# Constants moved to GpSimd, xn and y written in place, and the two result stores exchanged, in a one-token attention and MLP kernel

## The chip, the cores and the metric

One core of a Trainium2 chip. The metric is the device time of one execution in microseconds (us). Runs are compared with runs of the kernel before made in the same rounds on the same chip. The four jobs below ran on three chips (8, 3, 0 and 0), so runs of different jobs are compared through their ratios to the kernel before. Verdicts call a difference under 2% "same"; the differences here are about 1% at most, so what matters is the 95% interval of the ratio.

## The reference

One token `x` of 1024 values goes through a layernorm and then, side by side, through attention over the last 4096 positions of a cache (32 query heads, 4 key/value heads of 128) and through an MLP that normalises again.

```python
x = A_x
xn = _layernorm(x, axis=-1)
return x + _A_ref(xn, A_k_cache, A_v_cache, A_wq, A_wo) + _B_ref(xn, B_w1, B_b1, B_w2, B_b2)
```

Everything is bf16. With one token there is little arithmetic; the weights and the cache, 39.85 MB, have to be read.

## The kernel before

Each engine has its own list, and semaphores join them. SyncE issues all large loads in one queue: wq, K0, K1, w1, K2, K3, V, then w2 and wo into buffers that become free. GpSimd makes constants, VectorE does the layernorms, TensorE multiplies. The buffers are placed in SBUF, the memory that holds them, in the order in which they are asked for: some 40 small ones, then three large ones that nearly all loads write. A load counts as landed when the last increment of its semaphore is recorded, at 95.72 us for the last load here. PSUM is the memory in which TensorE leaves its sums (`PS` in the traces).

```python
    XNT = sb("XNT", [128, 8], dt.float32)
    XNTb = sb("XNTb", [128, 8], dt.bfloat16)
    # ... (cut: small buffers)
    KV = sb("KV", [128, HKV * W + HKV * NBLK * DH], dt.bfloat16)
    # ... (cut: views of KV)
    W1 = sb("W1", [128, KC * F], dt.bfloat16)
    WA = sb("WA", [128, KC * NQ], dt.bfloat16)
```

The opening on VectorE, after the sums of x and x*x:

```python
    DVE.mark(dve.tensor_scalar(out=XNT[:, :], in0=XT16[:, 0:8],
                               scalar1=msx[:, 2:3], scalar2=msx[:, 7:8],
                               op0=ALU.subtract, op1=ALU.mult))
    dve_dep()
    d_xn = DVE.mark(dve.tensor_copy(XNTb[:, :], XNT[:, :]))
    dve_dep()
    dve.wait_ge(POOL.sem, c_z)
    d_xz = DVE.mark(dve.tensor_copy(XZ[:, 96:9 * 97 - 1:97], XNTb[:, :]))
```

And the end:

```python
    act.wait_ge(ACT.sem, a_out)
    act.dma_start(out_row[:, 0:512], OUT[0:1, :]).then_inc(s_out[0], 16)
    sp.wait_ge(DVE.sem, d_out)
    sp.dma_start(out_row[:, 512:1024], OUT[32:33, :]).then_inc(s_out[1], 16)
    act.wait_ge(s_out[0], 16)
    sp.wait_ge(s_out[1], 16)
```

Of the kernel before, what the change touches and what calls it, by code (L numbers as in the profile page):

```python
# [4 lines left out]
dt = mybir.dt  # L5
ALU = mybir.AluOpType
ACTF = mybir.ActivationFunctionType
AX = mybir.AxisListType
# [37 lines left out]
def bass_parallel_sum__sliding_block_cached__mixer_channel_mlp__decode_kernel(  # L46
# [17 lines left out]
    INV_D = 1.0 / D  # L64
# [3 lines left out]
    pe, dve, act, pool, sp = nc.tensor, nc.vector, nc.scalar, nc.gpsimd, nc.sync  # L68
# [12 lines left out]
    s_out = [nc.alloc_semaphore(f"s_out{n}") for n in range(2)]  # L81

    PE = Track(nc, "S_PE")
    DVE = Track(nc, "S_DVE")
    ACT = Track(nc, "S_ACT")
    POOL = Track(nc, "S_POOL")

    def sb(name, shape, dtype):
        return nc.alloc_sbuf_tensor(name, shape, dtype)

    identb = sb("identb", [128, 128], dt.bfloat16)
    identf = sb("identf", [128, 128], dt.float32)
    onesf = sb("onesf", [128, 128], dt.float32)
    SELI = sb("SELI", [128, 32], dt.float32)
    REPL = sb("REPL", [128, 128], dt.bfloat16)
    SEL = sb("SEL", [32, 512], dt.bfloat16)
# [4 lines left out]
    SEL2 = sb("SEL2", [4, 2], dt.bfloat16)  # L101
    XTT = sb("XTT", [128, 256], dt.bfloat16)
    XT16 = sb("XT16", [128, 16], dt.float32)
    msx = sb("msx", [128, 8], dt.float32)
    XNT = sb("XNT", [128, 8], dt.float32)
    XNTb = sb("XNTb", [128, 8], dt.bfloat16)
    YT16 = sb("YT16", [128, 16], dt.float32)
    msy = sb("msy", [128, 8], dt.float32)
    EXPW = sb("EXPW", [128, 1], dt.float32)
    YTb = sb("YTb", [128, 8], dt.bfloat16)  # L110
    TT = sb("TT", [128, 1024], dt.float32)
    QMASK = sb("QMASK", [128, 4], dt.float32)
    QDB = sb("QDB", [128, 128], dt.bfloat16)
# [6 lines left out]
    MX4 = sb("MX4", [1, 128], dt.float32)  # L120
# [2 lines left out]
    PT = sb("PT", [128, 1024], dt.bfloat16)  # L123
    XZ = PT[:, 0:9 * 97 - 1]
    YZ = sb("YZ", [128, 9 * 97 - 1], dt.bfloat16)
    SELB = sb("SELB", [8, 2 * 97], dt.bfloat16)
    SUMP = sb("SUMP", [128, 1], dt.float32)
    REC = sb("REC", [32, 1], dt.float32)
# [8 lines left out]
    OUT = KV[0:33, 4 * D:4 * D + 512]  # L137
# [4 lines left out]
    PS = nc.alloc_psum_tensor("PS", [128, 8 * 512], dt.float32)  # L142
# [10 lines left out]
    out_row = out.rearrange("b s n -> (b s) n")  # L153
# [32 lines left out]
    def ahead_of_barrier(engine, n):  # L186
# [13 lines left out]
    act.dma_start(B1R[:, :], b1_rows).then_inc(s_b1, 16)  # L200
    act.dma_start(XB[0:2, :], A_x.rearrange("b s (o n) -> (b s o) n", o=2)).then_inc(s_b2, 16)
    act.dma_start(XB[2:4, :], b2_rows).then_inc(s_b2, 16)
    DVE.mark(dve.memset(PS[:, 0:4 * 512], 0.0))

    POOL.mark(pool.memset(identf[:, :], 0.0))
    pool.wait_ge(POOL.sem, POOL.cnt)
# [1 line left out]
        out=identf[:, :], in_=identf[:, :],  # L208
        pattern=[[-1, 128]], compare_op=ALU.not_equal, fill=1.0,
        base=0, channel_multiplier=1))  # L210
    c_onesf = POOL.mark(pool.memset(onesf[:, :], 1.0))
    POOL.mark(pool.memset(identb[:, :], 0.0))
    pool.wait_ge(POOL.sem, POOL.cnt)
    c_identb = POOL.mark(pool.affine_select(
        out=identb[:, :], in_=identb[:, :],
        pattern=[[-1, 128]], compare_op=ALU.not_equal, fill=1.0,
        base=0, channel_multiplier=1))
    POOL.mark(pool.memset(SEL[:, :], 0.0))
    pool.wait_ge(POOL.sem, POOL.cnt)
    c_sel = POOL.mark(pool.affine_select(  # L220
        out=SEL[:, :].rearrange("h (q p) -> h q p", q=4),
        in_=SEL[:, :].rearrange("h (q p) -> h q p", q=4),
        pattern=[[-1, 4], [1, 128]], compare_op=ALU.not_equal, fill=1.0,
        base=0, channel_multiplier=-4))
# [4 lines left out]
        out=MASK[:, :], in_=MASK[:, :], pattern=[[-REP, HKV]], compare_op=ALU.is_ge, fill=0.0,  # L229
        base=0, channel_multiplier=1))  # L230
    pool.wait_ge(POOL.sem, POOL.cnt)
    c_mask = POOL.mark(pool.affine_select(
        out=MASK[:, :], in_=MASK[:, :], pattern=[[REP, HKV]], compare_op=ALU.is_ge, fill=0.0,
        base=REP - 1, channel_multiplier=-1))
# [2 lines left out]
    c_selb = POOL.mark(pool.affine_select(  # L237
        out=SELB[:, :].rearrange("r (n m) -> r n m", n=2), in_=SELB[:, :].rearrange("r (n m) -> r n m", n=2),
        pattern=[[-16, 2], [-1, 97]], compare_op=ALU.not_equal, fill=1.0, base=0, channel_multiplier=16))
    POOL.mark(pool.memset(XZ[:, :], 0.0))  # L240
    c_z = POOL.mark(pool.memset(YZ[:, :], 0.0))
    c_lq = POOL.mark(pool.memset(LQ[:, :], 0.0))
# [7 lines left out]
    def dve_dep():  # L250
        dve.wait_ge(DVE.sem, DVE.cnt)

    def moments(ms, T16):

        n = DVE.mark(dve.tensor_reduce(
            out=ms[:, 0:2],
            in_=PS[:, 7 * 512: 7 * 512 + 16].rearrange("p (a k) -> p a k", a=2),
            axis=AX.X, op=ALU.add))
        dve_dep()
        DVE.mark(dve.tensor_scalar(out=ms[:, 2:4], in0=ms[:, 0:2],  # L260
                                   scalar1=INV_D, scalar2=None, op0=ALU.mult))
        dve_dep()
        DVE.mark(dve.tensor_tensor(out=ms[:, 4:5], in0=ms[:, 2:3], in1=ms[:, 2:3], op=ALU.mult))
        dve_dep()
        v = DVE.mark(dve.scalar_tensor_tensor(
            out=ms[:, 5:6], in0=ms[:, 3:4], scalar=EPS, in1=ms[:, 4:5],
            op0=ALU.add, op1=ALU.subtract))
        act.wait_ge(DVE.sem, v)
        a = ACT.mark(act.activation(out=ms[:, 6:7], in_=ms[:, 5:6], func=ACTF.Sqrt))
        dve.wait_ge(ACT.sem, a)  # L270
        DVE.mark(dve.reciprocal(out=ms[:, 7:8], in_=ms[:, 6:7]))
        dve_dep()
        return n
# [4 lines left out]
                           in_=XR[:, :].rearrange("p (r k) -> p k r", k=KC)))  # L278
# [3 lines left out]
    d_xsq = DVE.mark(dve.tensor_tensor(  # L282
        out=XT16[:, 8:16], in0=XT16[:, 0:8], in1=XT16[:, 0:8], op=ALU.mult))
    pe.wait_ge(DVE.sem, d_xsq)
    pe.wait_ge(POOL.sem, c_onesf)
    pe_sum1 = PE.mark(pe.matmul(PS[:, 7 * 512: 7 * 512 + 16], lhsT=onesf[:, :], rhs=XT16[:, 0:16]))  # L286
    dve.wait_ge(POOL.sem, c_identf)
    DVE.mark(dve.tensor_reduce(out=SELI[:, :], in_=identf[:, :].rearrange("p (i c) -> p c i", i=4),
                               axis=AX.X, op=ALU.add))
    dve_dep()  # L290
    DVE.mark(dve.tensor_reduce(out=QMASK[:, :], in_=identf[:, :].rearrange("p (t c) -> p t c", t=4),
                               axis=AX.X, op=ALU.add))
    DVE.mark(dve.tensor_copy(REPL[:, :].rearrange("p (i c) -> p i c", i=4),
                                      SELI[:, :].unsqueeze(1).to_broadcast([128, 4, 32])))
    dve.wait_ge(POOL.sem, c_identb)
    DVE.mark(dve.tensor_tensor(out=SEL2[:, :], in0=identb[0:4, 0:2], in1=identb[0:4, 2:4], op=ALU.add))
    dve.wait_ge(PE.sem, pe_sum1)
    moments(msx, XT16)
    DVE.mark(dve.tensor_scalar(out=XNT[:, :], in0=XT16[:, 0:8],
                               scalar1=msx[:, 2:3], scalar2=msx[:, 7:8],  # L300
                               op0=ALU.subtract, op1=ALU.mult))
    dve_dep()
    d_xn = DVE.mark(dve.tensor_copy(XNTb[:, :], XNT[:, :]))
    dve_dep()
    dve.wait_ge(POOL.sem, c_z)
    d_xz = DVE.mark(dve.tensor_copy(XZ[:, 96:9 * 97 - 1:97], XNTb[:, :]))
    DVE.mark(dve.tensor_copy(YT16[:, 0:8], XNTb[:, :]))
    dve_dep()
    d_ysq = DVE.mark(dve.tensor_tensor(  # L309
        out=YT16[:, 8:16], in0=YT16[:, 0:8], in1=YT16[:, 0:8], op=ALU.mult))  # L310
    pe.wait_ge(DVE.sem, d_ysq)
    pe_sum2 = PE.mark(pe.matmul(PS[:, 7 * 512: 7 * 512 + 16], lhsT=onesf[:, :], rhs=YT16[:, 0:16]))  # L312
    dve.wait_ge(PE.sem, pe_sum2)
    moments(msy, YT16)
    act.wait_ge(ACT.sem, ACT.cnt)
    ACT.mark(act.activation(out=EXPW[:, 0:1], in_=msy[:, 6:7], func=ACTF.Exp))
    d_y = DVE.mark(dve.tensor_scalar(
        out=YTb[:, :], in0=YT16[:, 0:8], scalar1=msy[:, 2:3], scalar2=msy[:, 7:8],
        op0=ALU.subtract, op1=ALU.mult))
    dve_dep()  # L320
    d_yz = DVE.mark(dve.tensor_copy(YZ[:, 96:9 * 97 - 1:97], YTb[:, :]))
    d_zs = DVE.mark(dve.memset(PS[:, 4 * 512:6 * 512], 0.0))



# [17 lines left out]
    def turn_k(g):  # L343
# [7 lines left out]
        out=QDB[:, :].rearrange("p (t c) -> p t c", t=4),  # L351
# [3 lines left out]
    last = pe.matmul(PS[:, 6 * 512: 6 * 512 + 128], lhsT=REPL[:, :], rhs=QDB[:, :], start=True, stop=True)  # L355
    pe_qx = PE.mark(last)
    dve.wait_ge(PE.sem, pe_qx)
    dve.wait_ge(POOL.sem, c_lq)
    act.wait_ge(PE.sem, pe_qx)
    act.wait_ge(POOL.sem, c_lq)  # L360
    d_lq = a_lq = None
# [34 lines left out]
    pe.wait_ge(DVE.sem, d_lq)  # L396
    pe.wait_ge(ACT.sem, a_lq)

    pe.wait_ge(DVE.sem, d_zs)
    k_blocks = KT.rearrange("p (g n b j a) -> p g n b j a", g=HKV, n=2, b=16, j=4, a=32)  # L400
    q_blocks = LQ[:, 0:2048].rearrange("p (g j m) -> p g j m", g=HKV, j=4)
    with nc.Fori(0, HKV, 1, engines=TENSOR) as g:
# [21 lines left out]
    for j, nj in enumerate(WO_CHUNKS):  # L424
# [19 lines left out]
        scalar1=-SCALE, scalar2=None, op0=ALU.mult))  # L444
    pe.wait_ge(DVE.sem, d_mx4)
    pe_nmb = PE.mark(pe.matmul(
        PS[:, 7 * 512 + 128: 7 * 512 + 129], lhsT=MX4[0:1, :], rhs=onesf[0:1, 0:1]))
    dve.wait_ge(PE.sem, pe_nmb)
    d_nmb = DVE.mark(dve.tensor_copy(NMB[:, :], PS[:, 7 * 512 + 128: 7 * 512 + 129]))  # L449
    act.wait_ge(DVE.sem, d_nmb)  # L450
# [30 lines left out]


    pe.wait_ge(s_b2, 32)
    pe.wait_ge(DVE.sem, d_nmb)
    for n in range(2):
        pe.matmul(ACC[n], lhsT=SEL2[:, n:n + 1], rhs=XB[:, :], start=True, stop=False)
# [4 lines left out]
    dve.wait_ge(PE.sem, pe_tot)  # L491
    DVE.mark(dve.reciprocal(out=REC[:, :], in_=PS[0:32, 512:513]))
    dve_dep()
    dve.wait_ge(POOL.sem, c_mask)
    DVE.mark(dve.tensor_scalar(out=RM[:, :], in0=MASK[:, :], scalar1=REC[:, 0:1], scalar2=None, op0=ALU.mult))
    dve_dep()

# [35 lines left out]
    c = 0  # L533
# [34 lines left out]
    d_out = DVE.mark(dve.tensor_copy(OUT[32:33, :], ACC[1]))  # L568
    act.wait_ge(s_fin, 1)
    a_out = ACT.mark(act.activation(out=OUT[0:1, :], in_=ACC[0], func=ACTF.Copy))  # L570
    act.wait_ge(ACT.sem, a_out)
    act.dma_start(out_row[:, 0:512], OUT[0:1, :]).then_inc(s_out[0], 16)
    sp.wait_ge(DVE.sem, d_out)
    sp.dma_start(out_row[:, 512:1024], OUT[32:33, :]).then_inc(s_out[1], 16)
    act.wait_ge(s_out[0], 16)
    sp.wait_ge(s_out[1], 16)

    return nc

# [27 lines left out]
```

## Time and profile before

| | before |
|---|---|
| time, median of the first 3 runs | 99.29 us |
| span of the profile | 98.1 us |
| last load landed | 95.72 us |
| first q matmul | 12.49 us |

The page of the kernel before: span, then busy time of each engine with its share and its number of instructions, then DMA queues (packets, MB, time of the packets as a share of 16 engines' span).

```profile
span 98.1 us, 1063 instructions
PE 68.3 (70%) x330; PEld 32.2 (33%) x330; DVE 37.1 (38%) x57; ACT 5.8 (6%) x11; POOL 6.7 (7%) x19
...
q8 instruction: 1, 0.02, 0.1%
...
q14 instruction: 1, 0.01, 0.0%
```

No engine is busy for more than 70% of the span; the queue of loads, shown in the prediction, is for 95.8%. Look at the last line too, which is easily passed over: one packet of a queue of kind "instruction". The trace's record of it has 8 KB at 77.9 us.

The timeline of the kernel before around the first use of x (start, length, engine and line, operation, in brackets the wait before it):

```profile
6.22 1.90 POOL L242 MEMSET LQ<- 128x2176 bf16 x1
...
7.65 0.63 DVE L277 STREAM_TRANSPOSE XTT<-XR 128x256 bf16<-128x256 bf16 x1 [4.40 <-DMA XR<-in_A_x_dram]
8.31 0.17 DVE L280 CAST XT<-XTT 128x8 f32<-128x8 bf16 x1
...
12.49 16.87 PE L336 MATMUL PS<-WA,PT 128*97 x64
```

### The profile page before, as it was taken

To read this page: it belongs to the slowest core of one execution; us is meant where nothing else is said; L and a number is where in the kernel's file an instruction comes from. 1 tells how busy PE (TensorE), PEld (TensorE's weight loads), DVE (VectorE), ACT (ScalarE), POOL (GpSimd) and SP (SyncE) were. 2 spreads that over 40 slices of the span, in tenths; PEclk is the share of its full clock that TensorE was granted. 3 is DMA by queue.
4 is the path that set the end of the run, shared out by engine and by line. 5 is a ranking of instruction groups with operands and counts; after the bars stand their busy time and mean duration, and the time that the engine had idled before them with its cause. 6 is when DMAs were issued, how large, how long until landed. Compare 5 with 4: busy or idle time off the path is not lost.

```text
span 98.1 us, 1063 instructions
## 1 busy us (share of the span) xinstructions
PE 68.3 (70%) x330; PEld 32.2 (33%) x330; DVE 37.1 (38%) x57; ACT 5.8 (6%) x11; POOL 6.7 (7%) x19
## 2 busy tenths in 40 slices
PE   0002199999992039999999743199991999854991
PEld 0002154555541025666644311033330334211320
DVE  4308562000008999600999544971007000000002
ACT  0500060000002000000000004000000000000002
POOL 6893000000000000000000000000000000000000
PEclk9999999999999555999999999755899579998599
DMA  5999899999998999999999999889989898999950
GB/s 170 447 453 473 379 427 427 427 397 427 449 538 374 386 409 427 456 385 427 427 427 427 427 481 503 374 386 538 386 386 523 361 488 356 436 405 413 412 215 8
DMA packets 3494, 39.89 MB, mean 406 GB/s; under 512 B 402, under 2 KB 420, under 8 KB 932
## 3 DMA queue, kind: packets, MB, share of 16 engines
q1 hardware_dynamic: 3458, 39.85, 95.8%
q8 instruction: 1, 0.02, 0.1%
q10 hardware_dynamic: 34, 0.01, 0.1%
q14 instruction: 1, 0.01, 0.0%
HBM read 39.86 MB, written 0.00 MB: 406 GB/s over the span
## 4 chain that ended last, share of the span: by engine, by line
DMA 81%; DVE 10%; SPq 4%; PE 2%; issue 1%
DMA KV<-in_A_k_cache_dram 43%; DMA KV<-in_A_wo_dram 38%; DVE KV L345 9%; PE PS L406 2%; SPq L176 1%; SPq L160 1%; SPq L166 1%; SPq L427 1%; DVE KV L568 1%; PE PS L558 0%
## 5 line engine op out<-in xcount | busy, mean ns | idle before, releaser
L345 DVE STREAM_TRANSPOSE KV<-KV 128x4096 bf16<-128x4096 bf16 x4 | 17.5, 4424 | 5.8 <-DMA KV<-in_A_k_cache_dram 5.8
L336 PE MATMUL PS<-WA,PT 128*97 x64 | 16.9, 433 | 0.1
L389 PE MATMUL PS<-W,YZ 128*97 x64 | 13.8, 380 | 4.0 <-POOLq L248 4.0
L389 PEld LDWEIGHTS PS<-W,YZ 128*97 x64 | 8.6, 134 | 9.2 <-issue 5.6
L336 PEld LDWEIGHTS PS<-WA,PT 128*97 x64 | 9.1, 142 | 7.6 <-issue 3.0
L549 PE MATMUL PS<-W,OP 128*1 128x512 bf16 x56 | 8.1, 452 | 2.8 <-DMA W<-in_A_wo_dram 2.8
L505 PE MATMUL PS<-KV,PT 128*32 128x512 bf16 x32 | 9.9, 484 | 0.1
L568 DVE CAST KV<-PS 1x512 bf16<-1x512 f32 x1 | 0.7, 683 | 19.9 <-PE PS L558 19.9
L538 PE MATMUL PS<-WA,GT 128*1 128x512 bf16 x56 | 7.9, 451 | 0.0
L406 PE MATMUL PS<-KV,LQ 128*128 x32 | 7.2, 380 | 0.5 <-DVE KV L345 0.5
L286 PE MATMUL PS<-XT,onesf 128*128 128x16 f32 x2 | 0.6, 386 | 8.7 <-DVE XT L282 8.7
L348 DVE STREAM_TRANSPOSE TT<-PS 128x1024 f32<-128x1024 f32 x1 | 1.3, 1251 | 14.1 <-PE PS L336 14.1
L505 PEld LDWEIGHTS PS<-KV,PT 128*32 128x32 bf16 x32 | 3.7, 117 | 5.9 <-issue 4.0
L549 PEld LDWEIGHTS PS<-W,OP 128*1 128x1 bf16 x56 | 2.7, 96 | 8.1 <-issue 3.2
L406 PEld LDWEIGHTS PS<-KV,LQ 128*128 x32 | 3.1, 98 | 4.6 <-issue 1.6
L538 PEld LDWEIGHTS PS<-WA,GT 128*1 128x1 bf16 x56 | 2.7, 96 | 4.7 <-issue 2.5
L510 DVE TENSOR_TENSOR TT<-PS,RM 32x512 f32<-32x512 f32 x1 | 0.7, 679 | 7.2 <-PE PS L505 7.2
L286 PEld LDWEIGHTS PS<-XT,onesf 128*128 128x128 f32 x2 | 0.5, 313 | 8.7 <-DVE XT L282 8.7
L452 ACT ACTIVATE Pe<-PS,NMB 128x512 bf16<-128x512 f32 x2 | 1.3, 684 | 28.3 <-DVE NMB L449 28.3
L570 ACT ACTIVATE KV<-PS 1x512 bf16<-1x512 f32 x1 | 0.6, 587 | 30.7 <-PE PS L558 30.7
L312 PE MATMUL PS<-YT,onesf 128*128 128x16 f32 x2 | 0.6, 384 | 2.4 <-DVE YT L309 2.4
L277 DVE STREAM_TRANSPOSE XTT<-XR 128x256 bf16<-128x256 bf16 x1 | 0.6, 630 | 4.4 <-DMA XR<-in_A_x_dram 4.4
(92 smaller groups left out, 33.7 us busy)
## 6 DMA issues: line engine op xcount, KB each, us to landing
WA<-in_B_w_dram SPq DMA_DIRECT2D x2, 3584.0 KB, 40.5
WA<-in_A_wq_dram SPq DMA_DIRECT2D x2, 2048.0 KB, 18.1
KV<-in_A_k_cache_dram SPq DMA_DIRECT2D x4, 1024.0 KB, 32.9
KV<-in_A_v_cache_dram SPq DMA_DIRECT2D x4, 1024.0 KB, 37.0
W<-in_B_w_dram SPq DMA_DIRECT2D x1, 3584.0 KB, 32.4
W<-in_B_w_dram SPq DMA_DIRECT2D x2, 1792.0 KB, 38.0
W<-in_A_wo_dram SPq DMA_DIRECT2D x1, 3328.0 KB, 34.5
WA<-in_A_wq_dram SPq DMA_DIRECT2D x1, 3072.0 KB, 11.6
```

Of the source, the lines that this page charges most:

```text
L160: sp.dma_start(WA[:, a:b], wq_pm[:, a:b]).then_inc(s_wq[j], 16)
L286: pe_sum1 = PE.mark(pe.matmul(PS[:, 7 * 512: 7 * 512 + 16], lhsT=onesf[:, :], rhs=XT16[:, 0:16]))
L336: last = pe.matmul(PS[0:97, n * 512:(n + 1) * 512], lhsT=shifted(XZ, s)[:, bass.ds(k, 1), :], rhs=wq_rows[:, bass.ds(k, 1), s * 1024 + n * ...
L345: dve.transpose(out=KT[:, g * W:(g + 1) * W], in_=KT[:, g * W:(g + 1) * W]).then_inc(r_k, 1)
L348: DVE.mark(dve.transpose(out=TT[:, :], in_=PS[:, 0:1024]))
L389: last = pe.matmul(PS[0:97, (2 + n) * 512:(2 + n) * 512 + HW], lhsT=shifted(YZ, s)[:, bass.ds(k, 1), :], rhs=w1_rows[:, bass.ds(k, 1), c: ...
L406: last = pe.matmul(PS[:, (4 + n) * 512:(5 + n) * 512], lhsT=q_blocks[:, bass.ds(g, 1), j, :], rhs=k_blocks[:, bass.ds(g, 1), n, :, j, :], ...
L452: a_exp = ACT.mark(act.activation(out=Pe[:, n * 512:(n + 1) * 512], in_=PS[:, (4 + n) * 512:(5 + n) * 512], func=ACTF.Exp, scale=SCALE, bi ...
L505: last = pe.matmul(PS[0:32, 0:512].rearrange("p (g d) -> p g d", g=HKV), lhsT=PT[:, b * 32:(b + 1) * 32], rhs=Vb[:, b, :, :], start=(b == ...
L538: pe.matmul(ACC[n], lhsT=GT[:, c:c + 1], rhs=W2[:, c * D + n * 512: c * D + (n + 1) * 512], start=False, stop=False)
L549: pe.matmul(ACC[n], lhsT=OP[:, r:r + 1], rhs=wo_at(r, 1)[:, n * 512:(n + 1) * 512], start=False, stop=False)
L568: d_out = DVE.mark(dve.tensor_copy(OUT[32:33, :], ACC[1]))
```

## The change

The intent: VectorE's opening is a chain of small operations, so take some away. GpSimd makes QMASK and SEL2, 1/D is built into the matrix that sums, xn and y are written straight into their padded buffers, and two PSUM clears become one. At the end the queue that issues slower (SyncE's, 0.32 us in before; ScalarE's 0.25) gets the half that is ready first.

```diff
-    identb = sb("identb", [128, 128], dt.bfloat16)
-    onesf = sb("onesf", [128, 128], dt.float32)
+    meanf = sb("meanf", [128, 128], dt.float32)
 ...
-    XNT = sb("XNT", [128, 8], dt.float32)
-    XNTb = sb("XNTb", [128, 8], dt.bfloat16)
-    YTb = sb("YTb", [128, 8], dt.bfloat16)
 ...
+    XNTb = XZ[:, 96:9 * 97 - 1:97]
+    YTb = YZ[:, 96:9 * 97 - 1:97]
 ...
-    DVE.mark(dve.memset(PS[:, 0:4 * 512], 0.0))
+    d_ps = DVE.mark(dve.memset(PS[:, 0:6 * 512], 0.0))
 ... (cut: QMASK and SEL2 by memset and affine_select on GpSimd, off VectorE;
 ...  the scaling by 1/D out of moments())
-    DVE.mark(dve.tensor_scalar(out=XNT[:, :], in0=XT16[:, 0:8],
 ...
-    d_xn = DVE.mark(dve.tensor_copy(XNTb[:, :], XNT[:, :]))
 ...
-    d_xz = DVE.mark(dve.tensor_copy(XZ[:, 96:9 * 97 - 1:97], XNTb[:, :]))
 ...
+    dve.wait_ge(POOL.sem, c_lq)
+    d_xz = DVE.mark(dve.tensor_scalar(out=XNTb, in0=XT16[:, 0:8],
 ... (cut: the rest of this call; the same for y; d_zs, the second clear, gone)
-    act.wait_ge(ACT.sem, a_out)
-    act.dma_start(out_row[:, 0:512], OUT[0:1, :]).then_inc(s_out[0], 16)
-    sp.wait_ge(DVE.sem, d_out)
-    sp.dma_start(out_row[:, 512:1024], OUT[32:33, :]).then_inc(s_out[1], 16)
-    act.wait_ge(s_out[0], 16)
-    sp.wait_ge(s_out[1], 16)
+    sp.wait_ge(ACT.sem, a_out)
+    sp.dma_start(out_row[:, 0:512], OUT[0:1, :]).then_inc(s_out[0], 16)
+    act.wait_ge(DVE.sem, d_out)
+    act.dma_start(out_row[:, 512:1024], OUT[32:33, :]).then_inc(s_out[1], 16)
+    sp.wait_ge(s_out[0], 16)
+    act.wait_ge(s_out[1], 16)
```

More of the change, by code (lines that the diff above doesn't have):

```diff
@@ L210, in bass_parallel_sum__sliding_block_cached__mixer_channel_mlp__decode_kernel @@
         base=0, channel_multiplier=1))
-    c_onesf = POOL.mark(pool.memset(onesf[:, :], 1.0))
-    POOL.mark(pool.memset(identb[:, :], 0.0))
+    c_meanf = POOL.mark(pool.memset(meanf[:, :], INV_D))
+    POOL.mark(pool.memset(QMASK[:, :], 1.0))
     pool.wait_ge(POOL.sem, POOL.cnt)
-    c_identb = POOL.mark(pool.affine_select(
-        out=identb[:, :], in_=identb[:, :],
-        pattern=[[-1, 128]], compare_op=ALU.not_equal, fill=1.0,
+    POOL.mark(pool.affine_select(
+        out=QMASK[:, :], in_=QMASK[:, :], pattern=[[-32, 4]], compare_op=ALU.is_ge, fill=0.0,
         base=0, channel_multiplier=1))
+    pool.wait_ge(POOL.sem, POOL.cnt)
+    c_qmask = POOL.mark(pool.affine_select(
+        out=QMASK[:, :], in_=QMASK[:, :], pattern=[[32, 4]], compare_op=ALU.is_ge, fill=0.0,
+        base=31, channel_multiplier=-1))
     POOL.mark(pool.memset(SEL[:, :], 0.0))
@@ L239, in bass_parallel_sum__sliding_block_cached__mixer_channel_mlp__decode_kernel @@
         pattern=[[-16, 2], [-1, 97]], compare_op=ALU.not_equal, fill=1.0, base=0, channel_multiplier=16))
+    POOL.mark(pool.memset(SEL2[:, :], 0.0))
+    for o in (0, 2):
+        pool.wait_ge(POOL.sem, POOL.cnt)
+        c_sel2 = POOL.mark(pool.affine_select(
+            out=SEL2[:, :], in_=SEL2[:, :], pattern=[[-1, 2]], compare_op=ALU.not_equal, fill=1.0,
+            base=-o, channel_multiplier=1))
     POOL.mark(pool.memset(XZ[:, :], 0.0))
@@ L255, in moments @@
         n = DVE.mark(dve.tensor_reduce(
-            out=ms[:, 0:2],
+            out=ms[:, 2:4],
             in_=PS[:, 7 * 512: 7 * 512 + 16].rearrange("p (a k) -> p a k", a=2),
             axis=AX.X, op=ALU.add))
-        dve_dep()
-        DVE.mark(dve.tensor_scalar(out=ms[:, 2:4], in0=ms[:, 0:2],
-                                   scalar1=INV_D, scalar2=None, op0=ALU.mult))
         dve_dep()
@@ L284, in bass_parallel_sum__sliding_block_cached__mixer_channel_mlp__decode_kernel @@
     pe.wait_ge(DVE.sem, d_xsq)
-    pe.wait_ge(POOL.sem, c_onesf)
-    pe_sum1 = PE.mark(pe.matmul(PS[:, 7 * 512: 7 * 512 + 16], lhsT=onesf[:, :], rhs=XT16[:, 0:16]))
+    pe.wait_ge(POOL.sem, c_meanf)
+    pe_sum1 = PE.mark(pe.matmul(PS[:, 7 * 512: 7 * 512 + 16], lhsT=meanf[:, :], rhs=XT16[:, 0:16]))
     dve.wait_ge(POOL.sem, c_identf)
@@ L290, in bass_parallel_sum__sliding_block_cached__mixer_channel_mlp__decode_kernel @@
     dve_dep()
-    DVE.mark(dve.tensor_reduce(out=QMASK[:, :], in_=identf[:, :].rearrange("p (t c) -> p t c", t=4),
-                               axis=AX.X, op=ALU.add))
     DVE.mark(dve.tensor_copy(REPL[:, :].rearrange("p (i c) -> p i c", i=4),
                                       SELI[:, :].unsqueeze(1).to_broadcast([128, 4, 32])))
-    dve.wait_ge(POOL.sem, c_identb)
-    DVE.mark(dve.tensor_tensor(out=SEL2[:, :], in0=identb[0:4, 0:2], in1=identb[0:4, 2:4], op=ALU.add))
     dve.wait_ge(PE.sem, pe_sum1)
     moments(msx, XT16)
-    DVE.mark(dve.tensor_scalar(out=XNT[:, :], in0=XT16[:, 0:8],
-                               scalar1=msx[:, 2:3], scalar2=msx[:, 7:8],
-                               op0=ALU.subtract, op1=ALU.mult))
+    dve.wait_ge(POOL.sem, c_lq)
+    d_xz = DVE.mark(dve.tensor_scalar(out=XNTb, in0=XT16[:, 0:8],
+                                      scalar1=msx[:, 2:3], scalar2=msx[:, 7:8],
+                                      op0=ALU.subtract, op1=ALU.mult))
     dve_dep()
-    d_xn = DVE.mark(dve.tensor_copy(XNTb[:, :], XNT[:, :]))
-    dve_dep()
-    dve.wait_ge(POOL.sem, c_z)
-    d_xz = DVE.mark(dve.tensor_copy(XZ[:, 96:9 * 97 - 1:97], XNTb[:, :]))
-    DVE.mark(dve.tensor_copy(YT16[:, 0:8], XNTb[:, :]))
+    DVE.mark(dve.tensor_copy(YT16[:, 0:8], XNTb))
     dve_dep()
@@ L311, in bass_parallel_sum__sliding_block_cached__mixer_channel_mlp__decode_kernel @@
     pe.wait_ge(DVE.sem, d_ysq)
-    pe_sum2 = PE.mark(pe.matmul(PS[:, 7 * 512: 7 * 512 + 16], lhsT=onesf[:, :], rhs=YT16[:, 0:16]))
+    pe_sum2 = PE.mark(pe.matmul(PS[:, 7 * 512: 7 * 512 + 16], lhsT=meanf[:, :], rhs=YT16[:, 0:16]))
     dve.wait_ge(PE.sem, pe_sum2)
@@ L316, in bass_parallel_sum__sliding_block_cached__mixer_channel_mlp__decode_kernel @@
     ACT.mark(act.activation(out=EXPW[:, 0:1], in_=msy[:, 6:7], func=ACTF.Exp))
-    d_y = DVE.mark(dve.tensor_scalar(
-        out=YTb[:, :], in0=YT16[:, 0:8], scalar1=msy[:, 2:3], scalar2=msy[:, 7:8],
+    d_yz = DVE.mark(dve.tensor_scalar(
+        out=YTb, in0=YT16[:, 0:8], scalar1=msy[:, 2:3], scalar2=msy[:, 7:8],
         op0=ALU.subtract, op1=ALU.mult))
-    dve_dep()
-    d_yz = DVE.mark(dve.tensor_copy(YZ[:, 96:9 * 97 - 1:97], YTb[:, :]))
-    d_zs = DVE.mark(dve.memset(PS[:, 4 * 512:6 * 512], 0.0))
     pe.wait_ge(DVE.sem, d_xz)
@@ L357, in bass_parallel_sum__sliding_block_cached__mixer_channel_mlp__decode_kernel @@
     dve.wait_ge(PE.sem, pe_qx)
-    dve.wait_ge(POOL.sem, c_lq)
     act.wait_ge(PE.sem, pe_qx)
@@ L397, in bass_parallel_sum__sliding_block_cached__mixer_channel_mlp__decode_kernel @@
     pe.wait_ge(ACT.sem, a_lq)
-    pe.wait_ge(DVE.sem, d_zs)
     k_blocks = KT.rearrange("p (g n b j a) -> p g n b j a", g=HKV, n=2, b=16, j=4, a=32)
@@ L446, in bass_parallel_sum__sliding_block_cached__mixer_channel_mlp__decode_kernel @@
     pe_nmb = PE.mark(pe.matmul(
-        PS[:, 7 * 512 + 128: 7 * 512 + 129], lhsT=MX4[0:1, :], rhs=onesf[0:1, 0:1]))
+        PS[:, 7 * 512 + 128: 7 * 512 + 129], lhsT=MX4[0:1, :], rhs=identf[0:1, 0:1]))
     dve.wait_ge(PE.sem, pe_nmb)
@@ L483, in bass_parallel_sum__sliding_block_cached__mixer_channel_mlp__decode_kernel @@
     pe.wait_ge(s_b2, 32)
+    pe.wait_ge(POOL.sem, c_sel2)
     pe.wait_ge(DVE.sem, d_nmb)
@@ L493, in bass_parallel_sum__sliding_block_cached__mixer_channel_mlp__decode_kernel @@
     dve_dep()
-    dve.wait_ge(POOL.sem, c_mask)
     DVE.mark(dve.tensor_scalar(out=RM[:, :], in0=MASK[:, :], scalar1=REC[:, 0:1], scalar2=None, op0=ALU.mult))
```

## The prediction

> **What bounds the kernel now.** I read first the 40-slice table of the page, then the chain that ended last, then the stretches (busy time of each engine and DMA share in chosen windows), and last the timeline around the places that the change touches.
>
> The 40-slice table: each digit of DMA is the busy share of one slice of 2.45 us.
>
> ```profile
> DMA  5999899999998999999999999889989898999950
> q1 hardware_dynamic: 3458, 39.85, 95.8%
> ```
>
> The 16 DMA engines work from the first slice to the last but two, and all of it is one queue, the loads issued by SyncE: 39.85 MB. The chain that ended last, in order of time (start, length, what):
>
> ```profile
> 4.69 41.86 DMA KV<-in_A_k_cache_dram
> ...
> 46.57 8.78 DVE KV L345 x2
> ...
> 58.29 37.43 DMA KV<-in_A_wo_dram
> 95.72 0.04 issue
> 95.76 0.40 PE PS L558 x2
> ...
> 96.19 0.68 DVE KV L568
> ```
>
> The last two chunks of wo, 0.25 MB each, were issued from 57.45 on and landed at 95.7. No small load takes 37 us by itself; it stood in the queue behind what was issued before it. So the VectorE and TensorE pieces between the two DMA pieces are only nominally on the chain: they decide when the last loads are put into the queue, not when the queue reaches them. The stretches say the same (engines' busy time and counts, granted clock, DMA share, GB/s):
>
> ```profile
> 10.00:95.00 85.00, 66.83 (x324) 31.54 (x324) 32.32 (x45) 3.92 (x9) 0.00 (x0) 0.88 1.00 424
> 94.00:96.00 2.00, 1.73 (x16) 0.38 (x10) 0.00 (x0) 0.00 (x0) 0.00 (x0) 1.00 0.28 109
> ```
>
> A DMA share of 1.00 over 85 us at 424 GB/s; 39.85 MB at that rate are 94.0 us, and the stream starts about 1 us into the span and ends near 95. **The bound is the load stream**, then a tail of some 2.4 us: last landing 95.72, two matmuls, two evictions of PSUM, two result DMAs (called loads in the change's title; they are stores), their landing at 98.1. Only the tail and the bytes can move the time.
>
> [...] an operation on 128x8 takes 0.17 us and one on 128x1 takes 0.16. So removing small operations is worth 0.2 us each, if they are on a path. [...] In the trace SyncE waits 0.9 us for its result store; no part of the change shortens that.
>
> **Part 1: fewer VectorE instructions in the opening.** Eight rows of the instruction order fall away on VectorE by my count (the title says ten; the two scalings of the moments run twice, which may be counted otherwise). Durations from the timeline of before: two scalings by 1/D (0.17 each), QMASK reduce 0.29, SEL2 add 0.14, cast to XNTb 0.17, copy into XZ 0.19, copy into YZ 0.19: 1.32 us. The PSUM clear of 1024 columns (0.91 us at 14.38) joins the first clear, which grows from 1.76 us for 2048 columns to an estimated 2.64 (by columns); it then ends near 4.1, and x lands only at 7.65, so it is hidden.
>
> On the path from x to the first q matmul: the moments start when TensorE is done (9.35 plus 0.04) rather than after the SEL2 add (9.51): -0.12. One scaling, start to start 9.51 to 9.72: -0.21. YT's cast started at 11.36, and now follows xn directly, at 11.07: -0.29. Together -0.62 us, so the q matmuls start near 11.9 instead of 12.49 (TensorE runs the second moments' matmul ahead of them). y comes earlier by another 0.21 + 0.33: near 13.0 instead of 14.17.
>
> What becomes of these 0.6 us:
>
> ```profile
> 31.37 0.59 DVE L368 CAST LQ<-PS 32x128 bf16<-32x128 f32 x2 [0.32 <-PE PS L355]
> 32.00 8.77 DVE L345 STREAM_TRANSPOSE KV<-KV 128x4096 bf16<-128x4096 bf16 x2
> 35.88 4.46 PE L389 MATMUL PS<-W,YZ 128*97 x15 [4.04 <-POOLq L248]
> 46.57 8.77 DVE L345 STREAM_TRANSPOSE KV<-KV 128x4096 bf16<-128x4096 bf16 x2 [5.80 <-DMA KV<-in_A_k_cache_dram]
> ```
>
> The q phase ends up to 0.6 us earlier (29.36 before), and so do the first two K transposes. But TensorE then idles 4.04 us until w1 has landed (GpSimd only passes the landing on), and VectorE idles 5.80 us until K has landed. Both idles grow by 0.6 us and everything after them stays where it is. w2 is issued at 28.8 instead of 29.39 into a queue that is not empty: by then 23.4 MB have been issued (wq 8.39, K 4.19, w1 7.34, V 4.19 MB, less rounding), which is 55 us of work at 424 GB/s. **Worth at the end: 0.**
>
> **Part 2: GpSimd.** identb goes (1.62 to 2.21: 0.59 us); QMASK and SEL2 come, each one memset and two selects like MASK's (3.44 to 3.98: 0.54 us). Its last memset, LQ, ended at 8.12 and should now end near 8.6. VectorE's xn now waits for it and would be ready near 10.4: 1.8 us of slack. Worth 0; even if it failed, 5.8 us of idle would absorb it.
>
> **Part 3: the result stores swap queues.** Before:
>
> ```profile
> 96.18 0.59 ACT L570 ACTIVATE KV<-PS 1x512 bf16<-1x512 f32 x1 [30.67 <-PE PS L558]
> 96.19 0.68 DVE L568 CAST KV<-PS 1x512 bf16<-1x512 f32 x1 [19.89 <-PE PS L558]
> 96.80 0.25 ACTq L572 DMA_DIRECT2D out_dram<-KV  x1
> 96.90 0.32 SPq L574 DMA_DIRECT2D out_dram<-KV  x1
> ```
>
> SyncE's issue takes 0.32 us, ScalarE's 0.25, and SyncE had the half that is ready last. Swapped, SyncE starts at 96.80 and ends at 97.12; ScalarE starts at 96.90 and ends at 97.15. The later end goes from 97.22 to 97.15: -0.07 us if landing counts from the end of the issue, 0 if from its start. I chose -0.05.
>
> **Sum:** 0 + 0 - 0.05: 99.29 becomes 99.24 us.
>
> **Rivals.** (a) *The opening is on the path after all*: the 0.62 us arrive at the end. For it: the printed chain runs through VectorE transposes. Against: the idles of 4.04 and 5.80 us for landings, and a queue full for 85 us. It would make 98.6. (b) *TensorE becomes the bound of the tail*: between 90 and 92 the granted clock was 0.50, and the wo matmuls ran at 0.43 us a pair; if the low clock[...] fell differently, the last matmuls could end after the last landing. Against: before the last two pairs TensorE idled for DMA (0.28 us before the last), and the second half of its schedule is tied to landings that don't move. It would make 99.6 to 100. [...] (d) *A store from ScalarE's queue lands later*, that queue having been quiet since its four small loads of the opening, while SyncE's is in use: +0.1 to +0.3, giving 99.4 to 99.5. In before that store had a head start of 0.10 us, so its landing shows nowhere.
>
> **Range and chances.** Three runs of before lie within 0.08 us, so the range comes from the rivals: some of (a) or a better tail down to 99.0, (d) or a little of (b) up to 99.5. Faster by 2% needs 2 us, more than the whole removed VectorE time of 2.2 us less the grown clear, on a path that shows slack three times over: 1%. Slower by 2% would need the stream itself disturbed or (b) at its worst: 1%.
>
> **What the profile after should show.** The q matmuls starting near 11.9 and the first K transpose near 31.4; the idle before w1's matmuls up from 4.0 to about 4.6 and before the third K transpose from 5.8 to about 6.4; that transpose still near 46.6; the last landing still near 95.7; LQ's memset ending near 8.6; the later of the two issues of stores ending near 97.15. The prediction is wrong if the last landing itself moves by more than 0.2 us, if TensorE no longer waits for DMA before its last pair, or if the span ends more than 1.0 us after the last issue.

The sum came to 0 + 0 - 0.05 us, 99.29 becoming 99.24.

## The result, and the profile after

| | before | after |
|---|---|---|
| time, median of 4 runs each | 99.30 us | 99.66 us |
| lowest and highest | 99.22, 99.40 | 99.51, 99.80 |
| ratio | | 1.0036 (1.0016 to 1.0055) |
| last load landed, in the profiled run | 95.72 us | 95.65 us |

Ratios are the mean time of one kernel's runs over that of the other's of the same rounds, so not quite the ratio of the medians. The changed kernel is slower by 0.36 us, clear of noise, and outside the range of the prediction.

The page after:

```profile
span 98.1 us, 1058 instructions
PE 66.4 (68%) x330; PEld 31.7 (32%) x330; DVE 36.7 (37%) x49; ACT 5.8 (6%) x11; POOL 7.1 (7%) x23
...
DMA  5999999999999899999999999989998989999970
...
q1 hardware_dynamic: 3458, 39.85, 96.3%
q8 instruction: 1, 0.02, 0.1%
q10 hardware_dynamic: 34, 0.01, 0.1%
```

Two small things differ from the page before. The packets of the loads took 96.3% of the span instead of 95.8%, for the same number of packets and bytes. And the line of q14 is gone. The timeline after, in the opening and at the end:

```profile
6.88 1.91 POOL L250 MEMSET LQ<- 128x2176 bf16 x1
...
7.29 0.64 DVE L282 STREAM_TRANSPOSE XTT<-XR 128x256 bf16<-128x256 bf16 x1 [2.97 <-DMA XR<-in_A_x_dram]
7.96 0.85 DVE L285 CAST XT<-XTT 128x8 f32<-128x8 bf16 x1
...
12.24 16.19 PE L331 MATMUL PS<-WA,PT 128*97 x64
...
35.66 4.69 PE L383 MATMUL PS<-W,YZ 128*97 x12 [4.75 <-POOLq L256]
...
46.44 8.77 DVE L340 STREAM_TRANSPOSE KV<-KV 128x4096 bf16<-128x4096 bf16 x2 [6.61 <-DMA KV<-in_A_k_cache_dram]
...
96.12 0.68 DVE L561 CAST KV<-PS 1x512 bf16<-1x512 f32 x1 [20.70 <-PE PS L551]
96.73 0.32 SPq L565 DMA_DIRECT2D out_dram<-KV  x1
96.83 0.25 ACTq L567 DMA_DIRECT2D out_dram<-KV  x1
```

The q matmuls start 0.25 us earlier, not 0.62, and even that is not the change's doing: x landed 0.36 us earlier in this run. From its transpose to the first q matmul it is 4.95 us, before 4.84. What the removed operations saved went into the cast of x, which took 0.85 us instead of 0.17 and ended at 8.81, just after GpSimd's memset of LQ at 8.79. The waits for w1 (4.75 us, before 4.04) and for K (6.61, before 5.80) are longer, as foretold, but they vary from run to run: b_swap, a run below with the opening of before, has as long ones (the third column is the idle time before the group and what ended it):

```profile
L345 DVE STREAM_TRANSPOSE KV<-KV 128x4096 bf16<-128x4096 bf16 x4 | 17.5, 4424 | 6.5 <-DMA KV<-in_A_k_cache_dram 6.5
L389 PE MATMUL PS<-W,YZ 128*97 x64 | 14.7, 399 | 4.8 <-POOLq L248 4.8
```

Nothing in the span explains a loss: this profiled run took 99.57 us against 99.38 for that of before, with the same span. Part of the difference must lie outside the instructions that the profile counts, and part may be hidden because a single traced run is not the median. The record has the span of every run: the time exceeds it by 1.53 us on average in the four runs of the changed kernel, and by 1.25 us (median) in the eleven runs of before made with the first job. So most of the 0.36 us lies outside the span. To find its causes the parts were separated on the chip.

### The profile page after: what moved, and what is told of

It reads as the page before. It is cut to its first block, busy times and chain, and to the rows that moved or that the text cites. A ratio compares the mean times of both kernels' runs of the same rounds, so it can differ in the third digit from the quotient of the medians.

```text
span 98.1 us, 1058 instructions
## 1 busy us (share of the span) xinstructions
PE 66.4 (68%) x330; PEld 31.7 (32%) x330; DVE 36.7 (37%) x49; ACT 5.8 (6%) x11; POOL 7.1 (7%) x23
## 3 DMA queue, kind: packets, MB, share of 16 engines
q1 hardware_dynamic: 3458, 39.85, 96.3%
## 4 chain that ended last, share of the span: by engine, by line
DMA 71%; PE 22%; SPq 3%; issue 1%; DVE 1%; POOLq 0%
DMA KV<-in_A_wo_dram 38%; DMA W<-in_B_w_dram 33%; PE PS L383 15%; PE PS L399 7%; SPq L158 1%; SPq L164 1%; SPq L420 1%; DVE KV L561 1%; PE PS L551 0%; POOLq L256 0%
## 5 line engine op out<-in xcount | busy, mean ns | idle before, releaser
L383 PE MATMUL PS<-W,YZ 128*97 x64 | 14.7, 400 | 4.8 <-POOLq L256 4.8
L331 PE MATMUL PS<-WA,PT 128*97 x64 | 16.2, 420 | 0.1
L383 PEld LDWEIGHTS PS<-W,YZ 128*97 x64 | 9.1, 142 | 10.4 <-issue 7.1
L498 PE MATMUL PS<-KV,PT 128*32 128x512 bf16 x32 | 9.2, 456 | 0.1
L291 PE MATMUL PS<-XT,meanf 128*128 128x16 f32 x2 | 0.6, 386 | 9.1 <-DVE XT L287 9.1
L531 PE MATMUL PS<-WA,GT 128*1 128x512 bf16 x56 | 6.2, 379 | 0.0
L291 PEld LDWEIGHTS PS<-XT,meanf 128*128 128x128 f32 x2 | 0.5, 313 | 9.1 <-DVE XT L287 9.1
L201 DVE MEMSET PS<- 128x3072 f32 x1 | 2.6, 2618 | 0.6 <-issue 0.6
```

The costliest lines, as they stand in the source:

```text
L201: d_ps = DVE.mark(dve.memset(PS[:, 0:6 * 512], 0.0))
L291: pe_sum1 = PE.mark(pe.matmul(PS[:, 7 * 512: 7 * 512 + 16], lhsT=meanf[:, :], rhs=XT16[:, 0:16]))
L331: last = pe.matmul(PS[0:97, n * 512:(n + 1) * 512], lhsT=shifted(XZ, s)[:, bass.ds(k, 1), :], rhs=wq_rows[:, bass.ds(k, 1), s * 1024 + n * ...
L383: last = pe.matmul(PS[0:97, (2 + n) * 512:(2 + n) * 512 + HW], lhsT=shifted(YZ, s)[:, bass.ds(k, 1), :], rhs=w1_rows[:, bass.ds(k, 1), c: ...
L498: last = pe.matmul(PS[0:32, 0:512].rearrange("p (g d) -> p g d", g=HKV), lhsT=PT[:, b * 32:(b + 1) * 32], rhs=Vb[:, b, :, :], start=(b == ...
L531: pe.matmul(ACC[n], lhsT=GT[:, c:c + 1], rhs=W2[:, c * D + n * 512: c * D + (n + 1) * 512], start=False, stop=False)
```

## The experiments

Names beginning with a_ start from the changed kernel with the stores put back, those beginning with b_ from the kernel before; a_waits and a_both_swap keep the changed kernel's stores. All fifteen results were correct.

### First job: stores or opening?

a_noswap is the change without its last hunk. b_swap is that hunk alone on the kernel before. b_waits leaves the stores and exchanges only who waits for which; a_waits does so on the whole change:

```diff
-    act.wait_ge(s_out[0], 16)
-    sp.wait_ge(s_out[1], 16)
+    sp.wait_ge(s_out[0], 16)
+    act.wait_ge(s_out[1], 16)
```

> The changed kernel with the two result stores and their waits as before the change. Theory 'closing': the loss of 0.36 us comes from ScalarE being the last to finish; this run then is back at 99.2 to 99.35 us. Rival 'opening': the loss comes from the moved constants and the changed start of TensorE; this run then stays at 99.6 to 99.7.

> The kernel before with only the two result stores and their waits swapped. Theory 'closing': 99.5 to 99.7 us, the whole loss. Rival 'opening': 99.25 to 99.3, or a little less.

> The kernel before, stores where they were; only the two last waits are exchanged, so ScalarE waits for the store that SyncE issued last, and SyncE for ScalarE's. Theory 'closing' (which engine finishes last counts, not which queue stores): slower, 99.4 to 99.6 us. Rival 'queue' (a store issued by ScalarE lands or completes later): 99.3, unchanged.

> The changed kernel with the stores swapped, but the two last waits exchanged, so SyncE waits for the later store. Theory 'closing': back to 99.2 to 99.35 us. Rival 'queue': 99.6 to 99.7, as the whole change. Rival 'opening': 99.6 to 99.7 too.

| run | median | ratio to before (95%) |
|---|---|---|
| a_noswap | 99.61 | 1.0025 (1.0010 to 1.0039) |
| b_swap | 99.49 | 1.0015 (1.0003 to 1.0027) |
| b_waits | 99.49 | 1.0018 (1.0002 to 1.0034) |
| a_waits | 99.63 | 1.0026 (1.0014 to 1.0038) |

Neither theory had it alone. The change without the swap still loses 0.25%, and the swap, or just the exchange of the waits, loses 0.15 to 0.18%. a_waits missed its expected return to 99.3, but it equals a_noswap, as it should if the swap costs only through who waits last.

That part can be read exactly in the trace's records of semaphore updates. After the program a semaphore that the kernel doesn't use is counted up in passes of steps some 0.04 us apart. From the end of the program's last wait to the end of the first pass, in us:

```
last wait on SyncE:    before 0.284   a_noswap 0.285   a_waits 0.285
last wait on ScalarE:  after  0.432   b_swap   0.432   b_waits 0.431
```

The pass costs 0.147 us more whenever ScalarE finishes last. Its first update comes 0.109 us after ScalarE's last wait in before and in after alike, though SyncE ended 0.18 us later than ScalarE in the first and 0.19 us earlier in the second; so ScalarE seems to come first in the pass, and SyncE can be 0.18 us late almost for free (the pass then ends 0.46 us after ScalarE's last wait instead of 0.43). The stores themselves gained nothing: from the last load's landing to the last wait it is 2.414 us in before and 2.421 in after, although the later issue ended 0.13 us earlier (97.09 against 97.22), half of it because the whole tail was 0.07 us earlier. What stayed the same is the time from the start of the later issue to the last wait: 1.24 us in before and after, 1.23 to 1.25 in all 17 traces, whichever queue issued it.

### Second job: which part of the opening?

Comparing the six traces packet by packet gave a clue: where the changed opening is in, packets of 8 KB in the stretch of V (49 to 58 us) take 313 ns on average; without it every one takes 309. And the 8 KB instruction packet at 77 us is missing. The theory of this job tied the two together, and that was wrong. a_dvepad lengthens VectorE's list again; the other three each take one part of the change alone:

```diff
+    DPAD = sb("DPAD", [128, 16], dt.float32)
 ... (after y is written)
+    for i in range(16):
+        DVE.mark(dve.memset(DPAD[:, i:i + 1], 0.0))
```

> The changed kernel with the stores as before, and 16 clears of one unused column each added to VectorE in its idle stretch after y. Theory 'refill': in the kernel before one 8 KB instruction load (77.9 us) falls into the stream of loads, and in the changed kernel, whose VectorE list is shorter, it does not; with it gone the 16 DMA engines run with less spread and their packets take up to 12 ns longer. Padded, the instruction load returns near 77 us, 8 KB packets take 309 ns again in the V stretch, and the time is 99.25 to 99.4 us. Rival 'opening' (the earlier start of TensorE or GpSimd's longer list costs the time by another way): stays at 99.55 to 99.7.

> The kernel before with only the constants made by GpSimd (QMASK, SEL2, 1/D in the matrix of the mean): four VectorE instructions fewer, three GpSimd instructions more. Theory 'refill': 99.6 us if the instruction load at 77 us is gone, 99.3 if it is still there. Rival 'constants': 99.5 to 99.6 whatever the instruction load does.

> The kernel before with only xn and y written straight into their padded places: three VectorE instructions fewer. Theory 'refill': 99.6 us if the instruction load at 77 us is gone, 99.3 if it is still there. Rival 'direct': 99.5 to 99.6 whatever the instruction load does.

> The kernel before with only the two clears of PSUM merged into the first: one VectorE instruction fewer. Theory 'refill': 99.3 us with the instruction load at 77 us still there, 99.6 without it. Rival 'clear': 99.5 to 99.6 whatever the instruction load does.

| run | median | ratio to before (95%) | VectorE's list | instruction packet at | 8 KB packets |
|---|---|---|---|---|---|
| before | 99.31 | | 63 | 77.9 us | 309.0 ns |
| a_dvepad | 100.36 | 1.0104 (1.0091 to 1.0118) | 69 | 61.4 | 314.7 |
| b_consts | 99.12 | 0.9979 (0.9967 to 0.9990) | 60 | 99.2 | 309.0 |
| b_direct | 99.58 | 1.0028 (1.0013 to 1.0042) | 60 | 99.4 | 313.5 |
| b_psum | 98.77 | 0.9942 (0.9929 to 0.9955) | 62 | 97.6 | 309.0 |
| a_noswap | 99.61 (first job) | 1.0025 | 53 | none recorded | 312.5 |

The list is counted in the built programs, waits included, so the ten removed instructions are two waits and eight operations. Three of the four expectations missed, in an instructive way; the 99.6 us of b_direct came in, but both of its theories had foretold it. b_psum takes away a single VectorE instruction in an idle stretch and gains 0.58%. Two separate effects are visible:

* **The instruction packet.** In the runs that record it, the shorter VectorE's list, the later it comes: from 61.4 us at 69 instructions to 99.2 and 99.4 at 60. The lists of the other engines don't order it so: b_psum's page counts as many instructions as that of before on every other engine, and its packet comes at 97.6 us instead of 77.9. At 77 us it falls into the stream of loads; at 97.6 us, after the last load, it falls into the wait for the stores. The records of landings show what it does: each load ends with 16 increments of its semaphore, and the program waits for all of them. They arrive within 0.72 us for the second half of w2 in before and within 1.22 us for the next load, wo's first, and stay that far apart to the end. In a_dvepad the jump (0.58 to 1.23 us) comes with the load in flight at 61.4 us, and there the last increment comes 0.64 us after the fifteenth instead of 0.11. In b_psum there is no jump. The packet itself took only 0.33 us in a_dvepad; why the last increment falls back by more was not found. In b_consts and b_direct the packet comes while the program closes. The spans say that b_consts pays for it there: they average 97.6 us, as b_psum's 97.5 do, but its times exceed them by 1.53 us, those of b_psum by 1.26.
* **Slow packets,** whenever xn and y are written in place (b_direct, and all a_ runs so far: 312.5 to 314.7 ns, against 309.0), whatever the instruction packet does.

The page and the chain of b_psum, to be held against those of before:

```profile
span 97.6 us, 1062 instructions
...
q1 hardware_dynamic: 3458, 39.85, 96.2%
...
q14 instruction: 1, 0.01, 0.0%
```
```profile
58.72 36.50 DMA KV<-in_A_wo_dram
95.22 0.04 issue
```

The packet is still counted (q14), but the last load lands at 95.22 instead of 95.72. The line says that it is there, not when.

### Third job: addresses

Why should writing xn elsewhere slow the loads? It removes three small buffers, and all buffers after them move. The addresses in the built programs: KV begins at 38912 in before, at 38656 in b_consts (both multiples of 256, both fast), and at 38816 in b_direct, 38560 in after and 38624 in a_dvepad (all 32 modulo 64, all slow). W1 and WA follow at multiples of 256 from KV. So put the addresses back without an instruction, or move them without one:

```diff
+    PAD = sb("PAD", [128, 88], dt.float32)    # a_align: 352 bytes. b_off32: 32 bytes, b_off64: 64
     KV = sb("KV", [128, HKV * W + HKV * NBLK * DH], dt.bfloat16)
```

a_both adds to a_align nine clears of single columns of PAD on VectorE after y, for a list of 62.

> The changed kernel with the stores as before and an unused buffer of 352 bytes a partition ahead of the large buffers, which puts these back at the addresses they had before (KV at 38912, not 38560). No instruction differs. Theory 'address': the removed small buffers moved the targets of all loads to addresses of 32 modulo 64, and the loads' packets take longer for it; now 8 KB packets take 309 ns throughout, the last load lands near 95.1 us, and the time is 99.0 to 99.25. Rival 'direct' (writing xn and y in place, or the earlier q phase, disturbs the loads): as without the buffer, 99.5 to 99.7.

> The kernel before with an unused buffer of 32 bytes ahead of the large buffers (KV at 38944, 32 modulo 64). Theory 'address': packets as slow as in the changed kernel, 312 to 315 ns for 8 KB in the V stretch, and 99.7 to 100.3 us, as the instruction load at 77 us is still there too. Rival: 99.3, unchanged.

> The kernel before with an unused buffer of 64 bytes ahead of the large buffers (KV at 38976, 0 modulo 64 but 64 modulo 128). If the unit that matters is 64 bytes: 99.3 us with packets of 309 ns. If it is 128 or more: slow packets, 99.7 to 100.3.

> The changed kernel with the stores as before, the buffers at their old addresses, and 9 clears of one unused column each on VectorE in its idle stretch after y, so that its list has 62 instructions, as in the kernel before with only the PSUM clears merged (98.77 us). If the time is made of the addresses, the place of the instruction load and the closing, as claimed: instruction load near 97.6 us, while the stores land, last load near 95.15, and 98.65 to 98.9 us, though VectorE does more than in the changed kernel. If the list's length matters only through work: no better than the aligned one without the clears, 99.0 to 99.25.

| run | median | ratio to before (95%) | 8 KB packets | last load |
|---|---|---|---|---|
| a_align | 98.79 | 0.9945 (0.9929 to 0.9961) | 309.0 ns | 95.13 us |
| b_off32 | 100.17 | 1.0085 (1.0068 to 1.0102) | 314.5 | 96.52 |
| b_off64 | 100.12 | 1.0083 (1.0065 to 1.0100) | 313.0 | 96.31 |
| a_both | 98.79 | 0.9946 (0.9930 to 0.9962) | 309.0 | 95.02 |

The address theory holds in both directions: an unused buffer makes the changed kernel 0.8% faster (0.9945 against a_noswap's 1.0025, of another job), and one of 32 bytes makes the kernel before 0.85% slower. The pages and chains, first a_align, then b_off32:

```profile
span 97.5 us, 1058 instructions
...
q1 hardware_dynamic: 3458, 39.85, 96.4%
```
```profile
58.11 37.03 DMA KV<-in_A_wo_dram
95.13 0.04 issue
```
```profile
span 98.9 us, 1063 instructions
...
q1 hardware_dynamic: 3458, 39.85, 95.6%
```
```profile
58.32 38.20 DMA KV<-in_A_wo_dram
96.52 0.04 issue
```

A share must be multiplied by its span: 96.4% of 97.5 is 94.0 us of packets on each engine, 95.6% of 98.9 is 94.5. The lower share belongs to the slower stream. a_align was better than expected (99.0 to 99.25), because the traces, of which that of a_noswap was its fastest run, had shown only 0.5 us of the 0.8. a_both did not beat a_align: the nine clears neither cost nor gain.

### Fourth job: a single instruction, the unit, and the swap once more

a_plus1 is a_both with ten clears instead of nine:

```diff
-    for i in range(9):
+    for i in range(10):
```

> The version with 9 clears (98.79 us, 62 VectorE instructions) with a tenth clear of one column: 63, as many as the kernel before. Theory 'instruction load': this one instruction of some 0.1 us in an idle stretch brings the 8 KB load back to 77 to 78 us, into the stream of loads; the last load lands near 95.5 instead of 95.0 and the time is 99.2 to 99.45. Rival 'work' (the gain of the shorter lists lies in the order of the work, not in their length): 98.8, unchanged.

> The kernel before with an unused buffer of 128 bytes ahead of the large buffers (KV at 39040, 0 modulo 128, 128 modulo 256). If the unit that matters is 256 bytes: slow packets and 100.0 to 100.3 us, as with 32 and 64 bytes. If it is 128: 99.3 with packets of 309 ns.

> The version with 9 clears with the result stores and their waits swapped as in the change. Theory 'closing': 0.1 to 0.2 us slower than without the swap, 98.88 to 99.0, by the first pass of the closing semaphore ending 0.43 us after the last wait instead of 0.28. Rival 'none': 98.79, within 0.03.

| run | median | ratio to before (95%) | what the trace shows |
|---|---|---|---|
| a_plus1 | 99.36 | 1.0005 (0.9990 to 1.0019) | instruction packet at 77.0 us; last load 95.76 |
| b_off128 | 100.13 | 1.0088 (1.0073 to 1.0103) | 8 KB packets 313.7 ns; last load 96.27 |
| a_both_swap | 99.01 | 0.9961 (0.9946 to 0.9976) | packets 309 ns; first pass of the closing 0.435 us |

The tenth clear, in a stretch where VectorE idles, costs 0.57 us (99.36 against the 98.79 of a_both, measured in the third job on the same chip): the 8 KB packet goes back from 97.3 us in a_both to 77.0, and the spread of the landings from 0.46 to 1.20 us at wo's first load. Its chain:

```profile
58.14 37.62 DMA KV<-in_A_wo_dram
95.76 0.04 issue
```

An offset of 128 bytes is as slow as 32 (1.0088 and 1.0085), so of the addresses tried only multiples of 256 are at full speed (8 KB packets of 309 ns; at the others 312.5 to 314.7). And the swap again shows 0.15% (0.9961 against 0.9946, of the third job; this pair alone is not clear of noise), with its 0.15 us in the closing.

### The sum

In thousandths of the time before, each size from runs that differ in it alone, and with a second pair in brackets. Where the two runs are of different jobs, their ratios to before are compared:

| part | from | thousandths |
|---|---|---|
| VectorE's shorter list takes the instruction packet out of the stream | b_psum against before (a_both against a_plus1: -5.9) | -5.8 |
| the large buffers lose their 256-byte alignment | a_noswap against a_align (b_off32: +8.5) | +8.0 |
| ScalarE finishes last | a_both_swap against a_both (b_swap: +1.5) | +1.5 |
| sum | | +3.7 |
| measured | after against before | +3.6 |

The agreement to a tenth is luck: by the intervals of the runs the three sizes are uncertain by about 1.3, 2.2 and 1.2 to 2.2, their sum by about 3, and a third pair for the addresses gives less (b_direct against b_consts, both with the packet in the closing: +4.9). Still, three effects that the change was not made for account for the loss without the one that it was made for. That part measures zero directly, within about 2: b_psum has the opening of before and a_align the changed one, and they stand at 0.9942 and 0.9945.

The version to keep is a_align: the change with its buffers aligned and its stores as before, 98.79 us, 0.55% faster than the kernel before and 0.9% faster than the change. The removal of one clear alone (b_psum) does as well. Both stand only as long as the list's length keeps the packet out of the stream.

## Why the prediction was right or wrong, point by point

* **The load stream is the bound: right.** The last load is followed by a tail of 2.41 to 2.43 us in every version read, and the differences of half a microsecond and more lie mainly in the landing of the last load.
* **The earlier opening is worth 0: right in the number,** by b_psum and a_align, but not for the reason given. The forecast -0.62 us did not come: from x's transpose to the first q matmul it is 4.83 to 4.95 us in the eight traces with the whole changed opening, and 4.83 to 4.86 in the seven with the opening of before, b_psum among them. Writing in place alone does shorten it (b_direct, 4.58), the constants on GpSimd lengthen it (b_consts, 5.07). The waits that were to grow to 4.6 and 6.4 us did grow to 4.75 and 6.61, by luck: b_swap, with the old opening, has 4.77 and 6.51, and a_align, with the new one, 4.19 and 5.95. The slack itself is real: the q matmuls end anywhere between 27.5 and 29.4 us in the traces, and the wait for w1 (4.0 to 5.7 us) takes that up. One sum is off without consequence: the loads issued before w2 add up to 24.1 MB, not 23.4.
* **GpSimd: nearly right.** LQ's memset ended at 8.79, not 8.6. The slack of xn did hold, but an earlier operation was caught, the cast of x, which ran 0.68 us longer, to just after that memset. It comes from GpSimd's longer list: the cast took 0.72 to 0.86 us in all nine traces that have it (b_consts among them), and 0.17 to 0.19 in the other eight. Why the cast runs longer while GpSimd is at work no run shows. At the end it costs nothing.
* **"Only the tail and the bytes can move the time": this step failed,** and with it "Worth at the end: 0" for part 1 as a whole. The bytes were the same and the stream changed twice: through where the buffers lie (+0.8 us) and through how long VectorE's list is (-0.6 us). A third place, the closing after the last wait (+0.15 us), is in neither the tail nor the bytes. The prediction asked what the removed instructions do, and not what goes with them: their place in a list and the addresses of everything behind their buffers. It took the stream, 424 GB/s between 10 and 95 us, as given; the change did move it, both ways: the last load's 16 increments came within 0.35 us instead of 1.12, and 8 KB packets in the stretch of V took 313 ns instead of 309; the last landing shows the balance, 95.65 us against 95.72. The unit of 256 bytes is what the runs show; by what mechanism a target off it takes longer was not shown. Nor does a trace show what the instruction packet is for; what the runs show is its cost, 0.57 us (a_plus1 against a_both).
* **The stores, -0.05 us: wrong in sign.** The later issue did end earlier, but the landing counts from its start (1.24 us to the last wait in both), which is the prediction's own case for 0; and ScalarE as the last engine to finish costs 0.147 us in the closing, which it had not looked at. Rival (d) had the direction and about the size, 0.1 to 0.3 us (a guess, from no trace), by another mechanism: no store landed later, and exchanging the waits alone (b_waits) shows the loss.
* **Rival (b), the granted clock: no sign of it.** TensorE still waited 0.24 us for the last load.
* **The range, 99.0 to 99.5,** was missed by 0.16 us. The chances for "within 2%" were right. None of its three signs of being wrong showed in the profiled run: the last landing moved by 0.07 us, TensorE waited for its last pair, and the span ended 0.99 us after the last issue.

What stays open: the instruction packet is put down to VectorE because it follows that list's length alone; the trace names no engine for it. Why the runs of a_noswap scatter from 99.31 to 99.76 was not found, nor why its times exceed their spans by 1.40 us on average and those of a_waits by 1.43, though SyncE finishes last in both; 1.25 is usual for before, and a_align has 1.29. So about 0.1 us of the 0.8 put down to the addresses lies outside the span, where slow packets of loads do not explain it. And a_align, whose packet is not in the record at all, may owe its place to the same luck of length.

## What to carry to other kernels

In a kernel bound by its loads, look at what an edit does to the loads' addresses and to the length of the instruction lists before you count the operations that it saves; here the addresses were worth 0.8% (a_noswap against a_align) and one instruction 0.57 us (a_plus1 against a_both). Fix the alignment of the large buffers explicitly, here at 256 bytes, so that a removed small buffer can't move them. When an edit that should be worth nothing moves the time by half a per cent, compare the packets' durations, the spread of each landing's 16 increments, and the packets of instruction queues. An unused buffer or an idle instruction is a cheap experiment that tells such side effects from the edit itself.
